# Attention before a routed MoE: factors and gates taken from PSUM tile by tile, tail maxima from transposes, heads of a pair in turn, and a planner that knows a shared port

## The chip, the cores and the metric

One core of a Trainium2 chip runs the whole program in one launch. The metric is the device time in microseconds (us) of that core, as the median of the runs. Five engines work side by side and meet at semaphores: PE (TensorE, matmuls and transposes), DVE (VectorE), ACT (ScalarE), POOL (GpSimd) and SP (SyncE, which here only issues DMAs, one after the other). PE and the transposes write PSUM; the other data lies in SBUF.

## The reference, cut to what matters

```
q, k, v: (8, 8, 576, 64)                 # batch, head, position, width
q_s = softmax(q, axis=-1)                # exp(q - max) / sum over the width
k_s = softmax(k, axis=2)                 # exp(k - max) / sum over the positions
kv  = einsum('bhsd,bhse->bhde', k_s, v)
x   = einsum('bhsd,bhde->bhse', q_s, kv) # then reshaped to 4608 tokens x 512
logits = x @ w_gate                      # 8 experts; every token goes to one, 576 per expert, best logits first
out = relu(x[mask] @ w1[e]) @ w2[e]      # per expert
h = out @ w_in; g = h * tanh(softplus(h)); result = g @ w_out
```

## The kernel before, in words

The program has three stages, each with an order of its own that a planner, `Sched`, writes out before anything runs. Every piece of work is an `op` with an engine, a cost in us, the keys it reads and writes, the buffers it takes (`new`) and a priority. `run` simulates the engines: it takes again and again the op that can start first (the priority settles ties), and emits it. So each engine's queue is in the planned order, and on the chip each engine works strictly down its queue. SP's DMA issues are planned in the same way, as engine "DMA".

Stage one is `attention`, with routing for the first expert at its end. Stage two runs the eight experts, stage three the last two matrices. The change is in `Sched`, in `attention`, in one flag of `route` and in three costs of `load_x`.

`attention` goes over the 8 batches b. Of the 576 positions of a head, 512 lie as 128 partitions x 4 rows r; the last 64 (the tail) of two batches share one tile. For each batch:

- `k_side`: `mx1` (L238, DVE) takes the maximum over the four rows of k, in two halves of 4 heads. `mx2` (L243, DVE) joins the tail's values, SBUF with SBUF, on 64 partitions. `tr` (PE) transposes, `red` (L253, DVE) reduces to the maximum over the partitions, `bc` (PE) spreads it, `cp` (ACT) copies it to SBUF. `sub` and `subh` (L269, L274, POOL) subtract it from k and `ex`, `exh` (ACT) take exp in place.
- `kv_side`: `mm` multiplies k with v for each head h, main part (L322) and tail (L315). Even heads write PSUM partitions 0 to 63, odd heads 64 to 127. The main loop does all four rows of one head, then those of the next. `norm` (L329 to L335, DVE) divides by the sums, `tr` (L341), `cp` and `gate` (L350) multiply by the gate's weights, so that KV has 128 columns of values, 16 of gates and 2 that give q's sums.
- `q_side`: `mx` (L374, DVE), `sub` (L380, POOL) and `ex` (ACT) for q. Then 36 tiles of 128 tokens, 4 a batch and one more for each pair of tails: `tr` (L394, PE), `cp` (L403, ACT) to `xs`, `mm` (L410, L413, PE) into the PSUM tile `xp`, of which there are two. `take` (L420, ACT) copies the 18 columns of gates and sums to SBUF and `copy` (L441, ACT) the 128 x 4 values to `xs`. When all four tiles of a group are there, `logits` makes the factor R (L426 add, L427 reciprocal), multiplies the gates by it (L429) and sums them into L (L433), all on DVE. `scaled` (L437) multiplies `xs` by R in place, the 18 odd tiles on DVE and the 18 even ones on POOL; `store` (L446, L450) sends two tiles at a time to DRAM (`xd`).

The PSUM tag "mT" has two buffers for everything but the q tiles and xp. k has 3 buffers, q three half-batch ones. All loads and stores are issued by SP in planned order, so a store that waits for its tiles holds the loads behind it.

The routing of the first expert (`route`, `round`) takes L in three pieces (tiles 0 to 17, 18 to 29, 30 to 35; `sel_first`, L625 on, `digits`, `cmp` L833), then six rounds of counting between DVE and PE. POOL then issues the indirect loads of the first expert's weights (L901) and the gathers of its tokens from `xd` (`load_x`, L929), which PE transposes.

Of the kernel before, what the change touches and what calls it, by code (L numbers as in the profile page):

```python
# [40 lines left out]
class Sched:  # L41
# [8 lines left out]
    def op(self, eng, cost, fn, r=(), w=(), prio=0, new=(), lat=None, slack=0.0):  # L50
# [21 lines left out]
        self.ops.append((eng, cost, fn, deps, prio, [k for _, k in new], lat, slack))  # L72
        return i
# [6 lines left out]
    def run(self, free=()):  # L80
# [17 lines left out]
        def start(i, t):  # L98
            s = max(t, free.get(self.ops[i][0], 0.0))
            for k in self.ops[i][5]:  # L100
                a = avail[self.kind[k]]
                if not a:
                    return None
                s = max(s, min(a))
            return s

        while ready:
# [4 lines left out]
            if self.keep and self.ops[i][4] >= self.urgent and self.ops[i][0] in ("DVE", "ACT"):  # L112

                end = key[i][0] + self.keep * self.ops[i][1]
                soon = [key[j] for j in key if self.ops[j][0] == self.ops[i][0] and self.ops[j][4] < self.urgent
                        and key[j][0] < end]
                if soon:
                    i = min(soon)[2]
            s = key[i][0]
            eng, cost, fn, deps, prio, new, lat, _ = self.ops[i]  # L120
# [6 lines left out]
            free[eng] = e  # L127
            done = e + (lat if lat is not None else 2.53 if eng == "DMA" else self.lat)
# [13 lines left out]
def attention(tc, nc, cst, q, k, v, w_gate, xs, L, R, xd, route):  # L142
# [12 lines left out]
            "qT": 2, "xp": 2, "km": 1, "dg": 2, "ms": 3, "gs": 3}  # L155
    sc = Sched(SLOT, 0.298)
# [21 lines left out]
    def load_k(b):  # L178
# [10 lines left out]
        for hh in range(2):  # L189
            sc.op("DMA", 1.5, lambda hh=hh: part(hh), w=[("k", b, hh)] + ([("kk", b)] if hh == 0 else []),  # L190
                  new=[("k", ("kk", b))] if hh == 0 else [], prio=0)
# [3 lines left out]
    def load_v(b):  # L195
# [13 lines left out]
        for hh in range(2):  # L209
            sc.op("DMA", 1.9, lambda hh=hh: part(hh), w=[("v", b, hh)] + ([("vv", b)] if hh == 0 else []),  # L210
                  new=[("v", ("vv", b))] if hh == 0 else [], prio=0)
# [3 lines left out]
    def load_q(b):  # L215
# [10 lines left out]
        for hh in range(2):  # L226
            sc.op("DMA", 1.5, lambda hh=hh: part(hh), w=[("q", b, hh)], new=[("q", ("q", b, hh))], prio=0)
# [4 lines left out]
    def k_side(b):  # L232
# [54 lines left out]
        for hh in range(2):  # L287
            sc.op(DVE, 1.25, lambda hh=hh: mx1(hh), r=[("k", b, hh), kk], w=[km], new=[("km", km)] if hh == 0 else [], prio=p)
        sc.op(DVE, 0.72, mx2, r=[kh, km], w=[km, khx], prio=p)
        sc.op(PE, 0.45, tr, r=[km], w=[mT], new=[("mT", mT)], prio=p)  # L290
        sc.op(DVE, 0.72, red, r=[mT], w=[dg], new=[("dg", dg)], prio=p)
        sc.op(PE, 0.45, bc, r=[dg], w=[mb], new=[("mT", mb)], prio=p)
        sc.op(ACT, 0.62, cp, r=[mb], w=[ms], new=[("ms", ms)], prio=p)
        for hh in range(2):
            sc.op(POOL, 2.45, lambda hh=hh: sub(hh), r=[ms, kk, ("k", b, hh)], w=[("k", b, hh)], prio=p)
            sc.op(ACT, 1.08, lambda hh=hh: ex(hh), r=[kk], w=[("k", b, hh)], prio=p)
        sc.op(POOL, 1.45, subh, r=[ms, kh, khx], w=[khx], prio=p)
# [3 lines left out]
    def kv_side(b):  # L301
# [5 lines left out]
        def mm(h0, h1, tail):  # L307
# [3 lines left out]
            for h in range(h0, h1):  # L311
                a, i = h % 2, h // 2
                c = slice(a * 64, a * 64 + 64)
                if tail:
                    nc.tensor.matmul(pt[c, i, 1:66], T["kh", b // 2][o:o + 64, h, :],  # L315
                                     T["vh", b // 2][o:o + 64, h, :], start=False, stop=(h >= 6),
                                     skip_group_check=True)
                    continue

                for r in range(4):  # L320
                    at = (0, 65, 129, 194)[r]
                    nc.tensor.matmul(pt[c, i, r % 2:r % 2 + 65], T["k", b, h // HH][:, h % HH, r, :],  # L322
                                     T["v", b, h // HH][:, h % HH, at:at + 65],
                                     start=(h == a and r == 0), stop=False, skip_group_check=True)
# [42 lines left out]
    def q_side(b):  # L367
# [47 lines left out]


        def take(r, r0, n):
            if r == r0:
                T["gs", b, r0] = wk.tile([128, 4, 4, KVW - 128], F32, name="gs", bufs=3)
            nc.scalar.activation(T["gs", b, r0][:, r - r0], T["xp", b, r][:, :, 128:KVW], AF.Copy)  # L420

        def logits(r0, n):
            g = T["gs", b, r0][:, 0:n]
            j = j_of(r0)
            rs = R[:, j:j + n]
            nc.vector.tensor_scalar(rs, g[:, :, :, 16:18], EPS, None, op0=OP.add)  # L426
            nc.vector.reciprocal(rs, rs)  # L427
            G = wk.tile([128, 4, 8, E], F32, name="G")
            nc.vector.tensor_tensor(G[:, 0:n].rearrange("p r (i a) e -> p (r i) a e", i=4),  # L429
                                    g[:, :, :, 0:16].rearrange("p r i (a e) -> p (r i) a e", a=2),  # L430
                                    rs.rearrange("p r i a -> p (r i) a")[:, :, :, None].to_broadcast([128, 4 * n, 2, E]),
                                    op=OP.mult)
            nc.vector.tensor_reduce(L[:, j:j + n, :], G[:, 0:n].rearrange("p r x e -> p r e x"), axis=AX, op=OP.add)  # L433

        def scaled(eng, r):
            x = part(r).rearrange("p i (a d) -> p (i a) d", a=2)
            eng.tensor_tensor(x, x, R[:, j_of(r)].rearrange("p i a -> p (i a)")[:, :, None].to_broadcast([128, 8, D]),  # L437
                              op=OP.mult)

        def copy(r):  # L440
            nc.scalar.activation(part(r), T["xp", b, r][:, :, 0:128], AF.Copy)  # L441

# [9 lines left out]
        for u in range(2 + b % 2):  # L452
# [3 lines left out]
            sc.op(POOL, 0.4 + 0.8 * n, lambda u=u: sub(u), r=[m], w=[qk], prio=p)  # L456
            sc.op(ACT, 0.2 + 0.45 * n, lambda u=u: ex(u), r=[qk], w=[qe], new=[("qe", qe)], prio=p)
        groups = [(0, 4)] if b < 7 else [(0, 2), (2, 2)]
        for r0, n in groups + [(4, 1)] * (b % 2):
            gs, L_ = ("gs", b, r0), [("L", j_of(r0) + i) for i in range(n)]  # L460
            for r in range(r0, r0 + n):
# [6 lines left out]
                sc.op(ACT, 0.26, lambda r=r, r0=r0, n=n: take(r, r0, n), r=[xp], w=[gs], new=[("gs", gs)] if r == r0 else [],  # L468
                      prio=p + 3.11)
                sc.op(ACT, 0.62, lambda r=r: copy(r), r=[xp], w=[x], prio=p + 3.74)  # L470
            sc.op(DVE, 0.6 + 0.2 * n, lambda r0=r0, n=n: logits(r0, n), r=[gs], w=[("R", b, r0)] + L_, prio=p + 3.11)
            for r in range(r0, r0 + n):
                x = ("x", b, r)
                if j_of(r) % 2:
                    sc.op(DVE, 0.75, lambda r=r: scaled(nc.vector, r), r=[("R", b, r0)], w=[x], prio=1000)
                else:
                    sc.op(POOL, 1.1, lambda r=r: scaled(nc.gpsimd, r), r=[("R", b, r0)], w=[x], prio=1000)
            for s0 in range(r0, r0 + n, 2):
                m = min(2, n)
                sc.op("DMA", 0.7 * m, lambda s0=s0: store(s0), r=[("x", b, r) for r in range(s0, s0 + m)], prio=3000)  # L480
# [104 lines left out]
class Moe:  # L585
# [17 lines left out]
    def route(self, ph, bank):  # L603
# [7 lines left out]
        def dve(cost, fn, r=(), w=(), early=False, slack=0.0):  # L611
            sc.op("DVE", cost, fn, r=[(x, ph) if isinstance(x, str) else x for x in r],
                  w=[(x, ph) if isinstance(x, str) else x for x in w], prio=0 if early else p, slack=slack)
# [309 lines left out]
    def load_x(self, ph, xd):  # L923
# [28 lines left out]
        for t in range(5):  # L952
            n = 128 if t < 4 else 64
            xg, tp, xt = ("xg", ph, t), ("tp", ph, t), ("xt", ph, t)
            sc.op("POOL", 1.1, lambda t=t, n=n: gather(t, n), r=[("ix", ph), "xd"], w=[xg], new=[("xg", xg)],
                  prio=p, lat=5.0 if ph else 2.5, slack=0.0 if ph else LISTS)
            sc.op("PE", 0.45, lambda t=t, n=n: tr(t, n), r=[xg], w=[tp], new=[("tp", tp)] if ph or t == 4 else [], prio=p)
# [672 lines left out]
```

## Time and profile before

| what | us |
|---|---|
| three runs | 1448.83, 1460.53, 1455.08; median 1455.08 |
| the profiled execution | 1457.38 |
| its span, first to last instruction | 1455.6 |

Busy shares over the span: PE 93%, DVE 74%, ACT 55%, POOL 19%. The profile's page cuts the span in 40 slices of some 36 us; the attention is the first four and a half. The windows view gives the same busy times for chosen stretches, the groups view sums instructions of a line, the timeline lists instructions in order with the idle time before each and what ended it. A row of the groups reads: line, engine, operation, output and inputs, count | busy us, mean ns | idle before.

### The profile page before, as it was taken

The page shows a single profiled execution, that of the slowest core. Times are in us where ns is not written, and L with a number is a line of the kernel's source. Part 1 is how long each engine was busy: PE and PEld are TensorE (multiplying, and loading weights), DVE is VectorE, ACT ScalarE, POOL GpSimd, SP SyncE. Part 2 cuts the span into 40 slices and gives each one's busy share as a digit, 9 for nine tenths or more (in the row PEclk, how much of TensorE's full clock was granted, in tenths as well). Part 3 has the DMA queues.
Part 4 walks back from the last instruction along what each step waited for, and adds up shares of the span by engine and source line. Part 5 has one row for each costly group of instructions (what it writes and reads, how often), then busy time and mean ns, then how long its engine had stood idle before and what let it go on. Part 6 is the DMA issues. An engine that isn't in the chain of part 4 may idle for free.

```text
span 1455.6 us, 26681 instructions
## 1 busy us (share of the span) xinstructions
PE 1350.2 (93%) x10240; PEld 1249.3 (86%) x10240; DVE 1073.7 (74%) x2144; ACT 798.8 (55%) x1558; POOL 273.0 (19%) x305
## 2 busy tenths in 40 slices
PE   4779469799999998999899999999999999999997
PEld 3668469699899997999799899998989999999896
DVE  8888876688688776763878677777768677786764
ACT  3458332343444435542766666666667666666663
POOL 8567241232232132100001000010101001010101
PEclk9899779899999998999999999999999999999999
DMA  9985442464565649767876566675657656665650
GB/s 274 226 232 175 166 149 90 129 187 147 159 225 163 201 151 301 251 211 266 301 275 207 170 222 190 201 239 168 208 177 250 200 164 215 196 226 175 192 178 29
DMA packets 161919, 286.98 MB, mean 197 GB/s; under 512 B 25600, under 2 KB 101376, under 8 KB 161792
## 3 DMA queue, kind: packets, MB, share of 16 engines
q1 hardware_dynamic: 137680, 222.35, 49.4%
q0 software_dynamic: 15040, 52.44, 10.9%
q10 hardware_dynamic: 9072, 10.49, 2.1%
q8 instruction: 81, 1.33, 0.4%
q14 instruction: 46, 0.38, 0.1%
HBM read 235.95 MB, written 49.28 MB: 196 GB/s over the span
## 4 chain that ended last, share of the span: by engine, by line
PE 44%; issue 39%; DVE 7%; DMA 4%; POOL 3%; ACT 2%; SPq 1%; another core or an unknown queue 0%; ACTq 0%; POOLq 0%; DVEq 0%
PE hp L971 13%; PE yp L990 13%; PE yp L1456 5%; PE hp L1330 5%; POOL out_dram L1468 2%; PE rt L845 2%; PE xp L410 1%; DMA wst<-in_moe_w_dram,wi 1%; PE kvp L322 1%; PE tp L940 1%; DVE km L238 1%; DMA wdi<-unit 1%; DVE G L429 1%; DMA yst<-yd 1%; PE qT L394 1%
## 5 line engine op out<-in xcount | busy, mean ns | idle before, releaser
L1456 PE MATMUL yp<-unit,g 128*128 128x512 f32 x1728 | 431.3, 392 | 0.1
L1456 PEld LDWEIGHTS yp<-unit,g 128*128 128x128 f32 x1728 | 309.9, 188 | 56.4 <-DVE g L1368 1.0
L1330 PEld LDWEIGHTS hp<-yTa,unit 128*128 128x128 f32 x2256 | 288.3, 188 | 18.6 <-DVE hp L1419 2.9
L1330 PE MATMUL hp<-yTa,unit 128*128 128x256 f32 x2256 | 294.1, 279 | 4.1 <-DVE hp L1419 2.7
L971 PE MATMUL hp<-xT,unit 128*128 128x288 f32 x1536 | 281.3, 303 | 7.8 <-DVE hh L982 7.6
L990 PE MATMUL yp<-hh,unit 128*128 128x288 f32 x1500 | 264.3, 297 | 0.5 <-issue 0.4
L971 PEld LDWEIGHTS hp<-xT,unit 128*128 128x128 f32 x1536 | 228.7, 191 | 9.4 <-DVE hh L982 8.2
L990 PEld LDWEIGHTS yp<-hh,unit 128*128 128x128 f32 x1500 | 220.8, 189 | 1.3 <-issue 0.9
L1468 POOL DMA_INDIRECT out_dram<-os,gix x36 | 39.5, 1098 | 786.8 <-ACT os L1464 453.7
L978 ACT ACTIVATE hh<-hp 128x288 fp32r<-128x288 f32 x125 | 51.1, 409 | 211.0 <-PE hp L971 179.3
L1338 ACT ACTIVATE u<-hp 128x512 f32<-128x512 f32 x144 | 85.9, 597 | 117.0 <-PE hp L1330 111.3
L1355 DVE SCALAR_TENSOR_TENSOR u<-w,r 128x512 f32<-128x512 f32 x144 | 98.8, 687 | 45.4 <-ACT r L1352 44.8
L1365 ACT ACTIVATE g<-w 128x512 fp32r<-128x512 f32 x144 | 90.3, 628 | 75.0 <-DVE w L1361 73.1
L901 POOL DMA_INDIRECT wst<-in_moe_w_dram,wi x64 | 67.7, 1058 | 277.8 <-DVE unit L888 76.3
L882 ACT ACTIVATE unit<-wst 128x512 fp32r<-128x512 f32 x128 | 77.7, 646 | 54.4 <-DMA wst<-in_moe_w_dram,wi 48.3
L982 DVE SCALAR_TENSOR_TENSOR hh<-hp,hh 128x288 fp32r<-128x288 f32 x125 | 56.7, 455 | 64.2 <-ACT hh L978 60.9
L1368 DVE TENSOR_TENSOR g<-w,g 128x512 fp32r<-128x512 f32 x144 | 98.8, 686 | 5.6 <-ACT g L1365 3.5
L1361 DVE SCALAR_TENSOR_TENSOR w<-r,hp 128x512 f32<-128x512 f32 x144 | 98.3, 684 | 5.5
L1330 PEld LDWEIGHTS hp<-yTb,unit 128*128 128x128 f32 x768 | 99.1, 191 | 3.6
L1330 PE MATMUL hp<-yTb,unit 128*128 128x256 f32 x768 | 102.1, 282 | 0.0
L1358 DVE SCALAR_TENSOR_TENSOR r<-u,r 128x512 f32<-128x512 f32 x144 | 98.8, 687 | 1.9
L1341 DVE TENSOR_SCALAR u<-u 128x512 f32<-128x512 f32 x144 | 61.2, 427 | 50.9 <-ACT u L1338 50.1
(203 smaller groups left out, 1767.9 us busy)
## 6 DMA issues: line engine op xcount, KB each, us to landing
unit<-wdi SPq DMA_DIRECT2D x216, 512.0 KB
unit<-wdi SPq DMA_DIRECT2D x72, 256.0 KB
wdi<-unit SPq DMA_DIRECT2D x56, 256.0 KB
yd<-ys ACTq DMA_DIRECT2D x15, 576.0 KB
k<-in_k_dram SPq DMA_DIRECT2D x16, 512.0 KB
q<-in_q_dram SPq DMA_DIRECT2D x16, 512.0 KB
v<-in_v_dram SPq DMA_DIRECT2D x32, 256.0 KB
xd<-xs SPq DMA_DIRECT2D x16, 512.0 KB
```

What stands on the lines that cost most here:

```text
L882: nc.scalar.activation(f, v, AF.Copy)
L971: MM(t, u[:, a, 128 * (f % 4):128 * (f % 4) + 128], x[:, b, k, HALF * hf:HALF * hf + HALF], start=(k == 0 and n == 0), stop=(k == 3 and n ...
L990: MM(T["yp", ph, hf][d], u[:, a, 128 * d:128 * d + 128], t[:, b], start=(f == 0 and n == 0), stop=(f == 7 and n == 2))
L1330: MM(dst, u[:, h, a, kk], y[:, b, kk], start=first, stop=False, skip_group_check=True)
L1338: nc.scalar.activation(t, T[zp], AF.Exp)
L1355: V.scalar_tensor_tensor(T[u], T[w], 1.0, T[rk], op0=OP.add, op1=OP.mult)
L1358: V.scalar_tensor_tensor(T[rk], T[u], 2.0, T[rk], op0=OP.subtract, op1=OP.mult)
L1361: V.scalar_tensor_tensor(T[w], T[rk], 0.5, T[zp], op0=OP.add, op1=OP.mult)
L1365: nc.scalar.activation(t[:, 0], T[w], AF.Copy)
L1368: V.tensor_tensor(T[g][:, 1], T[w], T[g][:, 0].bitcast(F32), op=OP.subtract)
L1456: MM(T["op", c, t], g[:, a, 128 * t:128 * t + 128], u[:, b], start=(i == 0 and n == 0), stop=(i == 15 and n == 2))
L1468: at = nc.gpsimd.indirect_dma_start(out=out, out_offset=bass.IndirectOffsetOnAxis(ap=gix[:, 4 * c + t:4 * c + t + 1], axis=0), in_=T["os", ...
```

## The change

Seven edits:

1. `take` moves from ACT to DVE and does a tile at a time, straight from PSUM: factor (add, reciprocal) and gates times factor, into a tile `G`. `logits` is only the sum.
2. The tiles whose number is a multiple of 4 (9 of 36) are also scaled by `take`, PSUM to `xs`, with no ACT copy. The other 27 are copied by ACT and scaled on POOL, none on DVE.
3. `mx2` is gone. Once per pair of batches PE transposes the tail tile (`trh`, buffer of tag "mT") and DVE reduces it (`redh`); `red` gets a second, small reduction over the two maxima.
4. `mm` of k and v takes the two heads of a pair in turn, row by row.
5. Stores of `xd` wait for the last batch's loads to have been issued and landed.
6. In `Sched`, ops marked `port` (POOL's subtractions and scalings, DVE's early routing) exclude each other in the plan, DVE and ACT ops may wait for a much more urgent one, and costs are corrected (`mx1` 1.25 to 1.95, loads 1.5 to 1.75, `mm` 2.0 to 1.1).
7. The last batch's tiles form groups (0, 1) and (2, 3, 4), the latter with priority -950; in `load_x` the first expert's gathers and transposes have other planned costs.

```diff
@@ Sched.run
+            if self.ops[i][8]:
+                s = max(s, free.get("port", 0.0))
...
-            if self.keep and self.ops[i][4] >= self.urgent and self.ops[i][0] in ("DVE", "ACT"):
+            limit = self.ops[i][4] - 500 if self.urgent is None else self.urgent
+            if self.keep and self.ops[i][4] >= limit and self.ops[i][0] in ("DVE", "ACT"):
...
+            if port:
+                free["port"] = e
@@ attention
-    sc = Sched(SLOT, 0.298)
+    sc = Sched(SLOT, 0.298, 1.0, None)
@@ k_side
-        def mx2():
-            m, o = T["km", b], (b % 2) * 64
-            nc.vector.tensor_tensor(m[o:o + 64], m[o:o + 64], T["kh", b // 2][o:o + 64], op=OP.max)
+        def trh():
+            t = T["hT", b // 2] = ps.tile([128, 4, 128], F32, name="hT", tag="mT", bufs=2)
+            m = T["kh", b // 2]
+            for i in range(4):
+                nc.tensor.transpose(t[:, i, :], m[:, 2 * i:2 * i + 2, :].rearrange("p a d -> p (a d)"), ident)
+        def redh():
+            t = T["m2", b // 2] = wk.tile([128, 4, 2, 2], F32, name="m2")
+            nc.vector.tensor_reduce(t[:, :, :, 1], T["hT", b // 2].rearrange("p i (o t) -> p i o t", o=2), axis=AX, op=OP.max)
...
-            nc.vector.tensor_reduce(t, T["mT", b], axis=AX, op=OP.max)
+            m = T["m2", b // 2][:, :, b % 2]
+            nc.vector.tensor_reduce(m[:, :, 0], T["mT", b], axis=AX, op=OP.max)
+            nc.vector.tensor_reduce(t, m, axis=AX, op=OP.max)
@@ kv_side
-            for h in range(h0, h1):
-                a, i = h % 2, h // 2
...
-                for r in range(4):
+            for i in range(h0 // 2, h1 // 2):
+                for r in (range(4, 5) if tail else range(4)):
+                    for a in range(2):
+                        h, c = 2 * i + a, slice(a * 64, a * 64 + 64)
@@ q_side
+        def early(r):
+            return j_of(r) % 4 != 0
-        def take(r, r0, n):
-            nc.scalar.activation(T["gs", b, r0][:, r - r0], T["xp", b, r][:, :, 128:KVW], AF.Copy)
+        def take(r, r0):
+            xp, rs = T["xp", b, r], R[:, j_of(r)]
...
+            V.tensor_scalar(rs, xp[:, :, 144:146], EPS, None, op0=OP.add)
+            V.reciprocal(rs, rs)
+            for o, at, n in ([] if early(r) else [(part(r), 0, D)]) + [(T["G", b, r0][:, r - r0], 128, E)]:
+                V.tensor_tensor(o if n == E else o.rearrange("p i (a d) -> p i a d", a=2),
+                                xp[:, :, at:at + 2 * n].rearrange("p i (a d) -> p i a d", a=2),
+                                rs[:, :, :, None].to_broadcast([128, 4, 2, n]), op=OP.mult)
...
-                if j_of(r) % 2:
-                    sc.op(DVE, 0.75, lambda r=r: scaled(nc.vector, r), r=[("R", b, r0)], w=[x], prio=1000)
+                if early(r):
+                    sc.op(ACT, 0.62, lambda r=r: copy(r), r=[xp], w=[x], prio=p + 3.74)
+                    sc.op(DVE, 0.55, lambda r=r, r0=r0: take(r, r0), r=[xp, G][:1 + (r > r0)], w=w, new=new, prio=first)
+                    sc.op(POOL, 1.1, lambda r=r: scaled(r), r=[rk], w=[x], prio=1000, port=True)
                 else:
-                    sc.op(POOL, 1.1, lambda r=r: scaled(nc.gpsimd, r), r=[("R", b, r0)], w=[x], prio=1000)
+                    sc.op(DVE, 1.25, lambda r=r, r0=r0: take(r, r0), r=[xp, G][:1 + (r > r0)], w=w + [x], new=new, prio=first)
...
-                sc.op("DMA", 0.7 * m, lambda s0=s0: store(s0), r=[("x", b, r) for r in range(s0, s0 + m)], prio=3000)
+                sc.op("DMA", 0.7 * m, lambda s0=s0: store(s0), r=[("x", b, r) for r in range(s0, s0 + m)]
+                      + [("in", B - 1, x, hh) for x in "kqv" for hh in range(2)], prio=3000)
```

## Rows read from the trace of the kernel before

**Rows 1.** Windows: us, busy (x) of PE, PEld, DVE, ACT, POOL; PEclk, DMA, GB/s.
```profile
6.00:70.00 64.00, 40.21 (x400) 35.61 (x400) 53.48 (x56) 26.87 (x46) 46.98 (x37) 0.87 1.15 267
6.00:163.50 157.50, 116.69 (x1279) 105.28 (x1279) 136.05 (x185) 91.36 (x176) 107.87 (x75) 0.92 0.85 223
163.50:204.50 41.00, 14.86 (x184) 12.19 (x185) 30.56 (x95) 8.64 (x16) 11.28 (x12) 0.56 0.50 164
204.50:1455.00 1250.50, 1218.61 (x8784) 1131.79 (x8780) 903.09 (x1835) 697.57 (x1366) 149.17 (x180) 0.99 0.61 195
```

**Rows 2.** Groups by line, DVE, from 6 to 163.5 us.
```profile
L238 DVE TENSOR_REDUCE km<-k 128x256 f32<-128x1024 f32 x16 | 30.7, 1942 | 4.9 <-DMA k<-in_k_dram 4.8
L429 DVE TENSOR_TENSOR G<-gs,R 128x256 f32<-128x256 f32 (+2 forms) x13 | 20.8, 1600 | 0.4
...
L437 DVE TENSOR_TENSOR xs<-xs,R 128x512 f32<-128x512 f32 x15 | 15.1, 1027 | 0.0
L243 DVE TENSOR_TENSOR km<-km,kh 64x512 f32<-64x512 f32 x8 | 9.1, 1132 | 0.2
L335 DVE TENSOR_TENSOR KV<-kvp,ks 64x256 f32<-64x256 f32 x16 | 6.8, 423 | 0.5
...
L426 DVE TENSOR_SCALAR R<-gs 128x32 f32<-128x32 f32 (+2 forms) x13 | 6.2, 476 | 2.7 <-ACT gs L420 2.7
L253 DVE TENSOR_REDUCE mx<-mT 128x4 f32<-128x512 f32 x8 | 5.5, 692 | 5.3 <-PE mT L249 4.9
L427 DVE RECIPROCAL R<-R 128x32 f32<-128x32 f32 (+2 forms) x13 | 3.8, 291 | 0.4
...
L329 DVE TENSOR_SCALAR ks<-kvp 128x8 f32<-128x8 f32 x8 | 1.3, 163 | 2.1 <-PE kvp L315 2.0
```

**Rows 3.** Timeline of DVE: start, us, engine, line, operation; stalled and free instances.
```profile
51.45 7.44 DVE L429 TENSOR_TENSOR G<-gs,R 128x256 f32<-128x256 f32 x1
...
80.95 5.69 DVE L429 TENSOR_TENSOR G<-gs,R 128x256 f32<-128x256 f32 x1
...
131.05 0.20 DVE L427 RECIPROCAL R<-R 128x8 f32<-128x8 f32 x1
131.29 0.23 DVE L429 TENSOR_TENSOR G<-gs,R 128x64 f32<-128x64 f32 x1
...
148.81 0.43 DVE L429 TENSOR_TENSOR G<-gs,R 128x256 f32<-128x256 f32 x1
```

**Rows 4.** Timeline of POOL, beside the second of those stalls.
```profile
81.69 4.67 POOL L269 TENSOR_TENSOR k<-k,ms 128x1024 f32<-128x1024 f32 x2
```

**Rows 5.** Timeline of PE: the two long gaps, and a main and a tail product.
```profile
65.26 1.09 PE L341 MATMUL kT<-ident,KV 128*128 128x128 f32 x4 [9.20 <-DVE KV L335]
...
97.23 1.09 PE L341 MATMUL kT<-ident,KV 128*128 128x128 f32 x4 [7.08 <-DVE KV L335]
...
114.65 1.55 PE L322 MATMUL kvp<-v,k 128*64 128x65 f32 x32
...
116.72 0.68 PE L315 MATMUL kvp<-vh,kh 64*64 64x65 f32 x16
```

**Rows 6.** SP's queue: its waits (total us, times, longest), and the last load issued.
```profile
SPq L219 <- ACT qe L387: 32.1, 10, 10.1
SPq L446 <- DVE xs L437: 19.7, 7, 5.7
...
135.51 0.38 SPq L219 DMA_DIRECT2D q<-in_q_dram  x1
```

**Rows 7.** Timeline of DVE where the last piece of routing begins.
```profile
163.34 0.68 DVE L437 TENSOR_TENSOR xs<-xs,R 128x512 f32<-128x512 f32 x1
...
167.14 0.35 DVE L833 TENSOR_TENSOR cm<-x,tab 128x384 bf16<-128x384 bf16 x1
```

**Rows 8.** Group by line, POOL, from 6 to 163.5 us.
```profile
L437 POOL TENSOR_TENSOR xs<-xs,R 128x512 f32<-128x512 f32 x18 | 20.4, 1150 | 10.7 <-DVE R L427 4.1 <-PE qT L394 3.4 <-ACT xs L403 2.1
```

**Rows 9.** Timeline of POOL: its first issue after the attention.
```profile
185.18 1.17 POOL L901 DMA_INDIRECT wst<-in_moe_w_dram,wi  x1 [22.58 <-DVE rk L706]
```

More of the change, by code (lines that the diff above doesn't have):

```diff
@@ L48, in __init__, with op @@
         self.touch, self.kind = {}, {}
-    def op(self, eng, cost, fn, r=(), w=(), prio=0, new=(), lat=None, slack=0.0):
+    def op(self, eng, cost, fn, r=(), w=(), prio=0, new=(), lat=None, slack=0.0, port=False):
         i = len(self.ops)
@@ L71, in op @@
         deps.discard(i)
-        self.ops.append((eng, cost, fn, deps, prio, [k for _, k in new], lat, slack))
+        self.ops.append((eng, cost, fn, deps, prio, [k for _, k in new], lat, slack, port))
         return i
@@ L119, in run @@
             s = key[i][0]
-            eng, cost, fn, deps, prio, new, lat, _ = self.ops[i]
+            eng, cost, fn, deps, prio, new, lat, _, port = self.ops[i]
             del ready[i]
@@ L189, in load_k @@
         for hh in range(2):
-            sc.op("DMA", 1.5, lambda hh=hh: part(hh), w=[("k", b, hh)] + ([("kk", b)] if hh == 0 else []),
+            sc.op("DMA", 1.75, lambda hh=hh: part(hh), w=[("in", b, "k", hh), ("k", b, hh)] + ([("kk", b)] if hh == 0 else []),
                   new=[("k", ("kk", b))] if hh == 0 else [], prio=0)
@@ L209, in load_v @@
         for hh in range(2):
-            sc.op("DMA", 1.9, lambda hh=hh: part(hh), w=[("v", b, hh)] + ([("vv", b)] if hh == 0 else []),
+            sc.op("DMA", 1.9, lambda hh=hh: part(hh), w=[("in", b, "v", hh), ("v", b, hh)] + ([("vv", b)] if hh == 0 else []),
                   new=[("v", ("vv", b))] if hh == 0 else [], prio=0)
@@ L226, in load_q @@
         for hh in range(2):
-            sc.op("DMA", 1.5, lambda hh=hh: part(hh), w=[("q", b, hh)], new=[("q", ("q", b, hh))], prio=0)
+            sc.op("DMA", 1.75, lambda hh=hh: part(hh), w=[("in", b, "q", hh), ("q", b, hh)], new=[("q", ("q", b, hh))], prio=0)
         if b % 2 == 1:
@@ L435, in scaled @@
[L435 to L438, printed above, removed]
+                T["G", b, r0] = wk.tile([128, 4, 4, 2, E], F32, name="G", bufs=3)
+            V = nc.vector
+            V.tensor_scalar(rs, xp[:, :, 144:146], EPS, None, op0=OP.add)
[4 more added lines that the diff above has]
+                                rs[:, :, :, None].to_broadcast([128, 4, 2, n]), op=OP.mult)
@@ L440, in copy, with scaled @@
+        def logits(r0, n):
+            nc.vector.tensor_reduce(L[:, j_of(r0):j_of(r0) + n, :],
+                                    T["G", b, r0][:, 0:n].rearrange("p r i a e -> p r e (i a)"), axis=AX, op=OP.add)
         def copy(r):
             nc.scalar.activation(part(r), T["xp", b, r][:, :, 0:128], AF.Copy)
+        def scaled(r):
+            x = part(r).rearrange("p i (a d) -> p (i a) d", a=2)
+            nc.gpsimd.tensor_tensor(x, x, R[:, j_of(r)].rearrange("p i a -> p (i a)")[:, :, None].to_broadcast([128, 8, D]),
+                                    op=OP.mult)
@@ L455, in q_side @@
             sc.op(DVE, 0.16 + 0.54 * n, lambda u=u: mx(u), r=[qk], w=[m], prio=p)
-            sc.op(POOL, 0.4 + 0.8 * n, lambda u=u: sub(u), r=[m], w=[qk], prio=p)
+            sc.op(POOL, 0.3 + 0.82 * n, lambda u=u: sub(u), r=[m], w=[qk], prio=p, port=True)
             sc.op(ACT, 0.2 + 0.45 * n, lambda u=u: ex(u), r=[qk], w=[qe], new=[("qe", qe)], prio=p)
-        groups = [(0, 4)] if b < 7 else [(0, 2), (2, 2)]
-        for r0, n in groups + [(4, 1)] * (b % 2):
-            gs, L_ = ("gs", b, r0), [("L", j_of(r0) + i) for i in range(n)]
+        groups = [(0, 4)] + [(4, 1)] * (b % 2) if b < 7 else [(0, 2), (2, 3)]
+        for r0, n in groups:
+            first = -950 if (b, r0) == (7, 2) else p + 3.11
+            L_ = [("L", j_of(r0) + i) for i in range(n)]
             for r in range(r0, r0 + n):
@@ L467, in q_side @@
                       new=[("xp", xp)], prio=p)
[L468 to L473, printed above, removed]
-                if j_of(r) % 2:
-                    sc.op(DVE, 0.75, lambda r=r: scaled(nc.vector, r), r=[("R", b, r0)], w=[x], prio=1000)
-                else:
-                    sc.op(POOL, 1.1, lambda r=r: scaled(nc.gpsimd, r), r=[("R", b, r0)], w=[x], prio=1000)
+                rk, G = ("R", b, r), ("G", b, r0)
+                new, w = [("G", G)] if r == r0 else [], [G, rk] if r == r0 else [("G", b, r0, r), rk]
+                if early(r):
+                    sc.op(ACT, 0.62, lambda r=r: copy(r), r=[xp], w=[x], prio=p + 3.74)
+                    sc.op(DVE, 0.55, lambda r=r, r0=r0: take(r, r0), r=[xp, G][:1 + (r > r0)], w=w, new=new, prio=first)
+                    sc.op(POOL, 1.1, lambda r=r: scaled(r), r=[rk], w=[x], prio=1000, port=True)
+                else:
+                    sc.op(DVE, 1.25, lambda r=r, r0=r0: take(r, r0), r=[xp, G][:1 + (r > r0)], w=w + [x], new=new, prio=first)
+            sc.op(DVE, 0.06 + 0.15 * n, lambda r0=r0, n=n: logits(r0, n), r=[("G", b, r0)] + [("G", b, r0, r) for r in range(r0 + 1, r0 + n)],
+                  w=L_, prio=first)
             for s0 in range(r0, r0 + n, 2):
-                m = min(2, n)
-                sc.op("DMA", 0.7 * m, lambda s0=s0: store(s0), r=[("x", b, r) for r in range(s0, s0 + m)], prio=3000)
+                m = min(2, r0 + n - s0)
+                sc.op("DMA", 0.7 * m, lambda s0=s0: store(s0), r=[("x", b, r) for r in range(s0, s0 + m)]
+                      + [("in", B - 1, x, hh) for x in "kqv" for hh in range(2)], prio=3000)
     def setup():
@@ L612, in dve @@
             sc.op("DVE", cost, fn, r=[(x, ph) if isinstance(x, str) else x for x in r],
-                  w=[(x, ph) if isinstance(x, str) else x for x in w], prio=0 if early else p, slack=slack)
+                  w=[(x, ph) if isinstance(x, str) else x for x in w], prio=0 if early else p, slack=slack, port=early)
         def pe(cost, fn, r=(), w=(), new=()):
```

58 lines of the change are left out of this document (24 added, 34 removed).

## The prediction

> **What bounds the kernel now.** I read the windows first, because the page's shares are a mean over three stages. From 204.5 us to the end PE is busy 1218.6 of 1250.5 us at a granted clock of 0.99 [rows 1]: nothing of the change is in there, so that stretch should move as a block. What can be won lies before it. From 163.5 to 204.5 runs the first routing, a chain between DVE and PE with neither full. From 6 us (the first k has landed) to 163.5 (the last logits are made) DVE is busy 136.1 of 157.5 us, PE 116.7, POOL 107.9, ACT 91.4 [rows 1]. So the attention is DVE's, with 21.4 us of idle time. The loads are close behind: up to 70 us the DMA engines are full, at 267 GB/s [rows 1].
>
> Then the groups of DVE in that stretch [rows 2], against single instances in the timeline [rows 3]. The product of gates and factors, L429, takes 20.8 us in 13 pieces; one of 128x256 took 7.44 us, another 5.69, a free one 0.43. What the long instances share is POOL: the 5.69 one runs from 80.95 to 86.64 and beside it POOL subtracts, without a break, from 81.69 to 86.36 [rows 4]. L335, of like size but with one input in PSUM, averages 0.42 over 16, so none of its instances was held long [rows 2]. A DVE operation with both tensors in SBUF waits for POOL's subtractions; one that reads PSUM does not. L426, L437 and L243 read SBUF alone and have means of 0.48, 1.03 and 1.13 [rows 2].
>
> Next PE's timeline, for what a stall does outside DVE. The two long L429 are followed by PE's longest gaps in the attention, 9.20 and 7.08 us, both ended by KV from L335, which stood in DVE's queue behind the stall [rows 5]. Last SP's queue: it waits 32.1 us for ACT to free q buffers and 19.7 us at stores of x for L437 on DVE, and the last q half is issued only at 135.5 [rows 6].
>
> **The change, part by part.** The sum is made on DVE's time in 6 to 163.5 us.
>
> Removed: L429 20.8, L426 6.2, L427 3.8, L437 15.1 and L243 9.1 us, together 55.0 [rows 2]. The sum into L stays as it is.
>
> Added by `take`, 36 times: an add from PSUM as L329 does it (0.16) [rows 2], a reciprocal of 128x8 (0.20) and a product of 128x64 [rows 3]. The trace has that product only from SBUF, 0.23 free [rows 3]; from PSUM the nearest is L335, four times as long a row on half the partitions, 0.42 [rows 2]. The term therefore lies between 36 x 0.59 = 21.2 and 36 x 0.78 = 28.1. I take 0.26, near the row of the same size: 36 x 0.62 = 22.3.
>
> Added for the 9 tiles scaled from PSUM: a pass over 128x512 of PSUM, L253's 0.69 [rows 2]: 6.2. Added for the tails: four reductions of 128x512 from PSUM, 4 x 0.69, and eight tiny ones at 0.16 (L329's, the smallest) [rows 2]: 4.1.
>
> Net on DVE: 55.0 - 22.3 - 6.2 - 4.1 = 22.4 us less. All that is added reads PSUM or is too short to meet POOL often, so I count no stalls in it. Bounds: with the dear product 16.6; above, one cannot tell how much of DVE's 21.4 us of idle goes too. It waits for transposes and late loads, and these wait for DVE. With half of it gone the gain is 33.
>
> Moved to PE: four transposes per pair, four times. One such set takes at most 1.09 us here (those right after a gap) [rows 5], so up to 4.4 us. Against it stands the order of heads. A main half is 32 instructions in 1.55 us, 48 ns each; the tail, which already takes the columns 0 to 63 and 64 to 127 in turn, 16 in 0.68, 43 ns each [rows 5]. In turn the half would cost 32 x 43 = 1.36, 0.19 less, 3 us in 16 halves; nothing is the other end. PE has 41 us of slack in the stretch [rows 1], so I cost PE's part at zero. The cover is DVE's load; were it gone, it would be 4.4 against 3.
>
> ACT loses 36 small copies and 9 large ones and is no bound. The stores behind all loads free SP from its 19.7 us at L446 [rows 6]; q loads then start earlier. I count 1 us, for DVE's idle time at late q only; the bounds are 0 and the half of the idle above. The stores themselves come late, in one run, but the first gather stands behind POOL's weight loads, which begin more than 20 us after the last logits [rows 9]. What they queue behind on SP is loads alone.
>
> After the last logits, three L437 stand between the routing's steps from 163.34 to 167.14 [rows 7]. They go: 3 x 0.60 (start to start) = 1.8.
>
> The planner's edits make no instruction cheaper. `mx1` was booked at 1.25 and takes 1.94 [rows 2], so the planned order was early by 0.7 us sixteen times over; a truer order serves the idle term, which I leave at nothing beyond that 1 us. The three costs in `load_x` move the order of the experts' stage: between -3 and +3, taken as 0, since PE is full there.
>
> Sum: 22.4 + 1.8 + 1.0 = 25.2 us. From the profiled 1457.4 that gives 1432.2; the median of the runs is 2.3 below the profiled execution, so 1430.
>
> **The rivals.**
>
> *POOL becomes the bound.* Nine more tiles of 1.15 us [rows 8] make 10.4 us. POOL's weight loads and gathers stand behind the scalings in its queue, and what it has not scaled by then it does beside the routing, whose SBUF operations wait for it as L429 did. For it: if POOL's 49.6 us of idle (157.5 - 107.9) stay, it ends at 163.5 + 10.4 = 173.9, while its first weight load, now at 185.2 [rows 9], is wanted at 160: 14 us late, 1444. Against it: most of that idle is spent waiting for DVE. The Trainium skill speaks against this edit: "GPSIMD Engine Reference", "Key points", has DVE about twice as fast on elementwise work, and says that the engines share SBUF interfaces, with contention for DVE instructions with two SBUF inputs. On the second the stalled L429 agrees; on the first the free L437 of 0.68 stands against POOL's 1.15 [rows 7, 8], 1.7 times.
>
> *The loads hold the end.* The last q half is issued at 135.5 because q buffers come free late [rows 6]. If that chain is not DVE's but its own, only the 28 us behind it shrink, by DVE's share 22.4 / 136: 4.6 + 1.8 = 6.4, 1449. Against it: ACT frees q after POOL's subtraction, which waits for DVE's maximum.
>
> *More than forecast.* DVE's idle time halves with the stalls: 33 + 1.8, 1420.
>
> *Slower: xp waits for DVE.* ACT emptied the gates from the two PSUM tiles; now DVE must, standing in a queue with the 1.94 us maxima [rows 2], and PE, in order, holds k's products behind the xp that finds no tile. If each of 36 tiles waits half a maximum, 0.97, that is 35 us on PE against 25 won: 10 slower, 1465. It decides from 0.7 us a tile. Against it: the plan places the takes with that wait in view, and DVE has less to do than before.
>
> *The turns of heads bring nothing.* The half stays at 1.55: no change in the sum, as PE has slack.
>
> **How the numbers follow.** A run can be told from no change here from about 1% (14.5 us). Forecast 0.62, own range 1420 to 1440; POOL 0.15 (half of it over the 1% line); loads 0.10 (over 6 us won, partly over 14.5); more than forecast 0.08; slower 0.05. Faster by over 1%: 0.60 + 0.07 + 0.06 + 0.08 = 0.81; slower 0.04; the rest, 0.15, within 1%. The range reaches from some 8 us below the 1420 case to just past POOL's: 1412 to 1446. It leaves out most of the loads case and the slower one.
>
> **What would show it.** Right: no DVE product over 1 us beside POOL but in the early routing; PE without gaps of 7 or 9 us; `take` at some 0.6 us a tile; the last logits near 139 us; the last q issued well before 135; the stretch from the first expert's products to the end still about 1250 us. Wrong: POOL still scaling when the routing's rounds begin, or its first weight load waiting for POOL itself; PE idle before L410 until DVE's take; or an experts' stage whose length has changed by over 5 us, since I count that as fixed.

## The result and the profile after

The changed kernel takes 1435.39 us (median of 6, 1432.10 to 1436.88) against 1454.76 for the kernel before (6 runs, the three of the table before and the profiled one among them): a ratio of 0.986, interval 0.9834 to 0.9885. The same kernel run again later gave 0.9863 (0.9835 to 0.9890). Forecast were 1430, in 1412 to 1446. The profiled execution is 1433.58 us, 23.8 under the profiled one of before; the sum had said 25.2.

The windows of the changed kernel, cut at the same events as [rows 1]: first k landed, last logits made, start of the experts' main stretch.

```profile
6.00:70.00 64.00, 48.24 (x557) 42.87 (x558) 49.13 (x78) 37.49 (x57) 52.05 (x41) 0.95 1.08 273
6.00:138.10 132.10, 109.54 (x1289) 98.67 (x1289) 106.70 (x236) 82.61 (x131) 111.02 (x82) 0.97 1.03 274
138.10:181.40 43.30, 15.06 (x190) 12.15 (x191) 32.76 (x104) 7.75 (x15) 11.56 (x13) 0.57 0.40 131
181.40:1431.50 1250.10, 1220.02 (x8779) 1133.36 (x8777) 902.57 (x1833) 699.12 (x1368) 149.82 (x180) 0.99 0.62 195
```

The attention went from 157.5 to 132.1 us, 25.4 less; the stretch behind it from 41.0 to 43.3; the rest stayed. DVE's busy time fell from 136.1 to 106.7 and its idle time rose, from 21.4 to 25.4. POOL, with 111 of 132 us, is now the busiest of the four.

DVE's groups in that window answer to [rows 2]:

```profile
L244 DVE TENSOR_REDUCE km<-k 128x256 f32<-128x1024 f32 x16 | 31.3, 1967 | 0.6 <-DMA k<-in_k_dram 0.3
...
L447 DVE TENSOR_TENSOR G<-xp,R 128x64 f32<-128x64 f32 x36 | 8.0, 221 | 0.9
L445 DVE RECIPROCAL R<-R 128x8 f32<-128x8 f32 x36 | 7.3, 203 | 1.2
L354 DVE TENSOR_TENSOR KV<-kvp,ks 64x256 f32<-64x256 f32 x16 | 6.8, 422 | 0.4
L447 DVE TENSOR_TENSOR xs<-xp,R 128x512 f32<-128x512 f32 x9 | 6.2, 691 | 0.5
...
L444 DVE TENSOR_SCALAR R<-xp 128x8 f32<-128x8 f32 x36 | 5.9, 163 | 9.6 <-PE xp L429 6.3 <-ACT xs L456 2.0 <-PE xp L432 1.3
...
L256 DVE TENSOR_REDUCE m<-hT 128x8 f32<-128x512 f32 x4 | 2.8, 692 | 2.5 <-PE hT L252 2.4
...
L268 DVE TENSOR_REDUCE mx<-m 128x4 f32<-128x8 f32 x8 | 1.3, 160 | 0.3
```

The three steps of a take sum to 0.59 us a tile, and no mean hides a stall: 36 products from PSUM at 0.22, where the group products of before took 20.8 us in 13 pieces.

PE's timeline, beside [rows 5]:

```profile
32.95 1.09 PE L252 MATMUL hT<-ident,kh 128*128 128x128 f32 x4 [3.83 <-DMA kh<-in_k_dram]
...
71.91 0.66 PE L360 MATMUL kT<-ident,KV 128*128 128x128 f32 x4 [0.34 <-DVE KV L354]
...
79.17 1.15 PE L341 MATMUL kvp<-v,k 128*64 128x65 f32 x32
...
97.88 0.63 PE L360 MATMUL kT<-ident,KV 128*128 128x128 f32 x4 [1.06 <-DVE KV L354]
```

The gaps of 9.20 and 7.08 us before `kT` are gone (the longest two now: 1.06 and 1.02). A new wait is there: the tails' transposes stand in PE's queue until their load lands. SP's queue, beside [rows 6]:

```profile
104.05 0.64 SPq L225 DMA_DIRECT2D q<-in_q_dram  x1
104.74 4.54 SPq L466 DMA_DIRECT2D xd<-xs  x4
```

The last q half is issued 31 us earlier. The stores start right behind it, before its data is used (DVE still waits for it up to 110.87): that stores wait for the last loads to have landed holds in the plan only. Where the attention hands over to the routing, on DVE, beside [rows 7]:

```profile
137.59 0.49 DVE L452 TENSOR_REDUCE L<-G 128x24 f32<-128x192 f32 x1
138.12 0.20 DVE L648 TENSOR_REDUCE v<-L 128x6 f32<-128x48 f32 x1
138.36 1.09 DVE L652 TENSOR_TENSOR t<-L,v 128x48 bf16<-128x48 f32 x1
...
141.41 0.24 DVE L648 TENSOR_REDUCE v<-L 128x12 f32<-128x96 f32 x1
...
143.84 0.56 DVE L856 TENSOR_TENSOR cm<-x,tab 128x768 bf16<-128x768 bf16 x1
```

The scalings between the routing's steps are gone. But the second piece (12 tiles) runs after the third (6 tiles); before, it lay ahead of the last logits. Its 3 us, 141.4 to 144.4, are most of why the stretch behind the attention grew. The rest is L652, which stands beside POOL's last scaling and takes 1.09 us, 0.9 more than the same step of the kernel before; less the 1.8 of the scalings that makes 2.1 of the 2.3. That step before the change:

```profile
164.17 0.21 DVE L629 TENSOR_TENSOR t<-L,v 128x48 bf16<-128x48 f32 x1
```

POOL, beside [rows 9]:

```profile
138.35 1.04 POOL L460 TENSOR_TENSOR xs<-xs,R 128x512 f32<-128x512 f32 x1 [0.70 <-ACT xs L456]
162.05 1.17 POOL L924 DMA_INDIRECT wst<-in_moe_w_dram,wi  x1 [22.66 <-DVE rk L729]
```

Its last scaling ends 1.3 us after the last logits; the weight loads wait for the routing, not for POOL.

### The profile page after: what moved, and what is told of

Its sections match the earlier page's. It is cut to its first block, busy times and chain, and to the rows that moved or that the text cites. A ratio compares the mean times of both kernels' runs of the same rounds, so it can differ in the third digit from the quotient of the medians.

```text
span 1431.8 us, 26732 instructions
## 1 busy us (share of the span) xinstructions
PE 1344.6 (94%) x10256; PEld 1244.2 (87%) x10256; DVE 1046.1 (73%) x2207; ACT 790.8 (55%) x1513; POOL 277.1 (19%) x314
## 4 chain that ended last, share of the span: by engine, by line
PE 55%; issue 30%; DMA 5%; DVE 5%; POOL 2%; ACT 2%; SPq 1%; ACTq 0%; POOLq 0%; DVEq 0%
PE hp L994 13%; PE yp L1013 12%; PE yp L1479 12%; PE hp L1353 11%; PE rt L868 2%; DMA kh<-in_k_dram 2%; POOL out_dram L1491 2%; DMA wst<-in_moe_w_dram,wi 2%; PE tp L963 1%; PE xp L429 1%; DMA xg<-xd,ix 1%; DVE km L244 1%; DMA v<-in_v_dram 1%; DMA q<-in_q_dram 0%; DVE cm L856 0%
## 5 line engine op out<-in xcount | busy, mean ns | idle before, releaser
L994 PE MATMUL hp<-xT,unit 128*128 128x288 f32 x1536 | 284.7, 303 | 4.2 <-DVE hh L1005 3.5
L1001 ACT ACTIVATE hh<-hp 128x288 fp32r<-128x288 f32 x125 | 51.3, 411 | 199.3 <-PE hp L994 183.3
```

What stands on the lines that cost most here:

```text
L994: MM(t, u[:, a, 128 * (f % 4):128 * (f % 4) + 128], x[:, b, k, HALF * hf:HALF * hf + HALF], start=(k == 0 and n == 0), stop=(k == 3 and n ...
```

## The experiments

All start from the changed kernel. Times of single stages are from one profile each. Three profiles with one and the same order of instructions, the changed kernel, its control and u_stores (see there), put the last logits at 138.1, 137.3 and 140.9 and the first expert product at 176.8, 176.5 and 179.8, so differences under some 4 us show nothing. x_psum, x_sbuf, u_plan and u_stores ran on one chip, the other experiments on a second one; the kernel before took 1461.98 us on the first and 1455.15 or 1452.87 on the second, so the ratios are the fairer measure.

| kernel | last logits, us | first expert product, us | ratio to before |
|---|---|---|---|
| before | 163.4 | 199.9 | 1 |
| changed | 138.1 | 176.8 | 0.986 (0.9834 to 0.9885) |
| u_take | 163.2 | 199.3 | 0.9984 (0.9963 to 1.0004) |
| u_take_port | 143.3 | 190.0 | 0.9939 (0.9920 to 0.9957) |
| u_tail | 139.5 | 177.3 | 0.9862 (0.9844 to 0.9881) |
| u_heads | 138.4 | 177.6 | 0.9866 (0.9849 to 0.9884) |
| x_psum | 138.9 | 178.0 | one run |
| x_sbuf | 156.5 | 195.5 | one run |
| u_plan | 143.7 | 178.8 | 0.9889 (0.9853 to 0.9924) |
| u_stores | 140.9 | 179.8 | 0.9867 (0.9840 to 0.9894) |
| v_less | 138.5 | 177.7 | one run |
| f_cut | 140.1 | 176.3 | 0.9879 (0.9854 to 0.9905) |
| f_cut3 | 142.7 | 178.9 | 0.9885 (0.9853 to 0.9916) |
| again (control) | 137.3 | 176.5 | 0.9863 (0.9835 to 0.9890) |

**u_take: factors and gates by group from SBUF again.**

```diff
-            V.tensor_scalar(rs, xp[:, :, 144:146], EPS, None, op0=OP.add)
+            nc.scalar.activation(T["gs", b, r0][:, r - r0], T["xp", b, r][:, :, 128:KVW], AF.Copy)
...
+                if j_of(r) % 2:
+                    sc.op(DVE, 0.75, lambda r=r: scaled(nc.vector, r), r=[("R", b, r0)], w=[x], prio=1000)
```

> The changed kernel with one part undone: gates and sums are copied to SBUF by ACT again, factors and gates are made for a whole group from SBUF, and 18 tiles are scaled on DVE in SBUF; the rest of the change stays, the planner's too, but it is not told that these DVE operations need the port. Theory (stalls of DVE operations with both tensors in SBUF beside POOL's subtractions): the group products of 128x256 take several us again where POOL works, DVE's busy time from 6 us to the last logits is 20 us or more above the changed kernel's 106.7, and the last logits come 12 to 25 us later than 138.1. Rival (the planner's order brought the gain, and the memory of the operands matters little): the products stay under 1 us and the last logits come within 5 us of 138.

Undoing this part (edits 1 and 2 together; no run separates them) undoes the whole gain: last logits at 163.2. The window up to there, with DVE busy 130.4 us against 106.7, and groups of DVE in it:

```profile
6.00:163.20 157.20, 121.67 (x1295) 110.92 (x1295) 130.37 (x180) 92.12 (x176) 107.62 (x74) 0.88 0.84 221
```

```profile
L244 DVE TENSOR_REDUCE km<-k 128x256 f32<-128x1024 f32 x16 | 31.0, 1956 | 1.8 <-DMA k<-in_k_dram 1.6
L455 DVE TENSOR_TENSOR xs<-xs,R 128x512 f32<-128x512 f32 x14 | 21.1, 1547 | 0.0
...
L444 DVE TENSOR_SCALAR R<-gs 128x32 f32<-128x32 f32 (+3 forms) x12 | 9.2, 766 | 7.4 <-ACT gs L438 7.3
L447 DVE TENSOR_TENSOR G<-gs,R 128x256 f32<-128x256 f32 (+3 forms) x12 | 7.7, 642 | 0.4
```

In one detail the expectation failed: the group products are not the long ones now (mean 0.64). The order differs, and the stalls fell on the scalings, 1.55 us a piece, and on the additions. Which SBUF product or addition meets POOL depends on the order; not every SBUF operation is held: the maxima of L244 take 1.96 us here as in the other kernels. The last q half leaves 17 us later than in the changed kernel:

```profile
121.50 0.37 SPq L225 DMA_DIRECT2D q<-in_q_dram  x1
```

**u_take_port: the same, with the planner told.**

```diff
-    sc.op(DVE, 0.6 + 0.2 * n, lambda r0=r0, n=n: logits(r0, n), r=[gs], w=[("R", b, r0)] + L_, prio=first)
+    sc.op(DVE, 0.6 + 0.2 * n, lambda r0=r0, n=n: logits(r0, n), r=[gs], w=[("R", b, r0)] + L_, prio=first, port=True)
```

(and the same on DVE's scalings.)

> As the kernel before it in this list, but the planner is told that the group products and the scalings on DVE exclude POOL's work. Theory (the stall itself costs, and PSUM is the way round it): told or not, DVE and POOL still need each other's time, so what DVE does not stall it waits in the plan: last logits 8 to 25 us after 138.1. Rival (knowing the port is enough): last logits within 5 us of 138.1 with the old products.

Each view has half. The last logits come 5.2 us late only, so a plan that keeps the two engines apart recovers 20 of 25 us, and making factors for a whole group, which this kernel shares with u_take, costs at most those 5.2 at the last logits. But what it kept apart it put off: twelve scalings ran on DVE between 150.9 and 171.9, during the routing, and the stores behind them. SP's queue:

```profile
157.62 14.89 SPq L464 DMA_DIRECT2D xd<-xs  x8
172.61 2.70 SPq L468 DMA_DIRECT2D xd<-xs  x2
```

and POOL's first gather of `xd`, which needs them all (the wait named is another DMA of that queue; the stores are what it reads):

```profile
180.97 0.95 POOL L950 DMA_INDIRECT xg<-xd,ix  x1 [11.45 <-DMA w<-in_moe_w_in_dram]
```

In the changed kernel that gather comes at 167.9. So of the 19.9 us that the plan won over u_take at the last logits, 9.3 are left at the first expert product (190.0 against 199.3).

**x_psum and x_sbuf: one product more in each take, equal but for the memory of one operand.**

```diff
+            V.tensor_tensor(wk.tile([128, 4, 2, E], F32, name="twice", bufs=1), xp[:, :, 128:144].rearrange("p i (a d) -> p i a d", a=2),
+                            rs[:, :, :, None].to_broadcast([128, 4, 2, E]), op=OP.mult)
```

In x_sbuf `wgbd`, of the same shape in SBUF, stands for `xp[:, :, 128:144]`.

> The changed kernel, same plan, with one more product in every take: the same 128x64 product of xp (PSUM) and factors, written a second time to a scratch tile that nobody reads. Both theories: 36 more of about 0.22 us, 8 us more of DVE busy time, last logits 0 to 5 us after 138.1. It is the control of the next kernel.

> The same with the scratch product's first operand in SBUF (the gate weights, the same shape), so that only the memory of one operand differs from the kernel before. Theory (a DVE operation with both tensors in SBUF waits for POOL's subtractions and scalings, and POOL is busy 111 of 132 us): the scratch products have a mean of 0.7 us or more where POOL works, DVE's busy time grows by over 20 us, and the last logits come 8 to 30 us after 138.1. Rival (the stalls came from something else, such as the broadcast factor): 0.22 us as in the control, and the same end.

The group of the added product in x_psum:

```profile
L450 DVE TENSOR_TENSOR twice<-xp,R 128x64 f32<-128x64 f32 x36 | 7.7, 213 | 0.0
```

and in x_sbuf:

```profile
L450 DVE TENSOR_TENSOR twice<-wgbd,R 128x64 f32<-128x64 f32 x36 | 28.5, 793 | 0.0
```

Same plan, same size, same count: 0.21 against 0.79 us. Single instances take 0.211 to 0.218 us in x_psum and 0.212 to 2.477 in x_sbuf. The end moves by 0.8 us in the one and by 18.4 in the other. The windows of both up to their last logits, x_psum first:

```profile
6.00:138.90 132.90, 109.33 (x1289) 98.21 (x1289) 110.53 (x272) 82.68 (x131) 111.02 (x82) 0.97 1.04 272
```

```profile
6.00:156.50 150.50, 119.26 (x1289) 107.24 (x1289) 131.08 (x273) 83.45 (x131) 111.20 (x82) 0.90 0.92 241
```

DVE's busy time grew by 24.4 us in x_sbuf, as expected, but by 3.8 in x_psum and not by 8: in the trace the added products partly overlap the instructions beside them. The pair shows the mechanism by itself: the product whose tensors both lie in SBUF waits for POOL, the one with an operand in PSUM does not.

**u_tail: the tails' maxima on DVE from SBUF again.**

```diff
+            nc.vector.tensor_tensor(m[o:o + 64], m[o:o + 64], T["kh", b // 2][o:o + 64], op=OP.max)
...
-            sc.op(PE, 0.45, trh, r=[kh], w=[hT, ("khx", b), ("khx", b + 1)], new=[("mT", hT)], prio=p)
```

> The changed kernel with the tails' maxima joined on DVE from SBUF again (eight of 64x512), no transposes of the tails. Theory by DVE's sum: 9.1 us removed and 4.1 added, so 5 us more busy time on DVE and last logits 2 to 6 us later. Rival (loads and PE set the end by now, DVE has slack): within 1.5 us of 138.1.

The window of u_tail up to the changed kernel's last logits:

```profile
6.00:138.10 132.10, 111.37 (x1264) 98.09 (x1264) 116.01 (x233) 81.72 (x130) 113.02 (x81) 0.96 1.03 273
```

DVE works 9.3 us more, where 5 were expected: the joined maxima cost 9.8 instead of 9.1, 1.9 are steps of the routing's second piece that now run ahead of the last logits, and the rest, on balance, is longer steps of the early routing. The end comes 1.4 us later and the first product 0.5: the rival. This part of the change is not worth anything that can be measured; PE no longer waits for the tails' loads in exchange.

**u_heads: one head after the other.**

```diff
-                for r in (range(4, 5) if tail else range(4)):
-                    for a in range(2):
+                for r, a in [(4, a) for a in range(2)] if tail else [(r, a) for a in range(2) for r in range(4)]:
```

> The changed kernel, same plan, but the products of k and v do all rows of one head before the next head. Theory of the prediction (PE has slack): each half goes from 1.08 back to 1.48 us, 6.4 us of PE in all, and the last logits move by under 1.5 us. Rival (PE, busy 109.5 of 132 us, now lies on the path): last logits 3 to 7 us later.

PE's timeline in u_heads, a main half:

```profile
74.74 1.55 PE L341 MATMUL kvp<-v,k 128*64 128x65 f32 x32
```

Heads in turn make the half 1.15 instead of 1.55 us. In u_heads PE's busy time in the window is 113.6 against 109.5, and the end moves by 0.3 us: nothing.

**u_plan: the planner without the port and without the wait for urgent operations.**

```diff
-    sc = Sched(SLOT, 0.298, 1.0, None)
+    sc = Sched(SLOT, 0.298)
...
-            if port:
-                free["port"] = e
```

> The changed kernel with the planner's port exclusion and its waiting for urgent operations taken out, costs and work as changed. Theory (what the chip executes counts; the takes read PSUM, so hardly anything on DVE meets POOL): last logits within 4 us of 138.1, the early routing's operations a little longer. Rival (the planner's knowledge carries the gain): 8 to 25 us later.

Between the two: last logits 5.6 us later. But here the routing's second piece comes before them, on DVE:

```profile
134.46 0.24 DVE L644 TENSOR_REDUCE v<-L 128x12 f32<-128x96 f32 x1
...
143.16 0.50 DVE L448 TENSOR_REDUCE L<-G 128x24 f32<-128x192 f32 x1
```

so the first expert product is only 2.0 us behind the changed kernel's, and the ratios' intervals overlap. Beside u_stores, the changed kernel's order on the same chip, the last logits come 2.8 us later and the first product 1.0 earlier: no effect is shown.

**u_stores: stores free to go among the loads.**

```diff
-                sc.op("DMA", 0.7 * m, lambda s0=s0: store(s0), r=[("x", b, r) for r in range(s0, s0 + m)]
-                      + [("in", B - 1, x, hh) for x in "kqv" for hh in range(2)], prio=3000)
+                sc.op("DMA", 0.7 * m, lambda s0=s0: store(s0), r=[("x", b, r) for r in range(s0, s0 + m)], prio=3000)
```

> The changed kernel with stores of xd free to go among the loads as soon as their tiles are ready. The prediction's step (SP frees 19.7 us, of which 1 us counts): last logits 0 to 2 us later. Rival (loads are the bound by now, 274 GB/s over the whole attention, and stores in between delay them): the last q half is issued 8 us or more after 104, and the last logits come 5 to 15 us later.

The last q load, SP's queue in u_stores:

```profile
105.53 0.45 SPq L225 DMA_DIRECT2D q<-in_q_dram  x1
106.03 4.65 SPq L466 DMA_DIRECT2D xd<-xs  x4
```

The first store still goes behind the last q: no store went among the loads. Instruction by instruction, every engine, SP too, has the order of the changed kernel. With the rest of the change in place the plan puts the stores there without being told, so this run decides neither the step nor the rival. It is a repeat of the changed kernel, and its 2.8 us at the last logits are the spread between repeats.

**v_less: fewer loads.** v is loaded for three batches only, its tails for four; later batches use old values, so the result is another.

```diff
-            for i in range(2):
+            for i in range(2 if b < NV else 0):
                 x = src(v, b, hh)
```

> The changed kernel, same plan, but v is loaded for the first three batches only (tails for the first four); the later batches use what lies in the buffers, so 5.8 of the 28.3 MB of input are not moved and the output is another. Theory (after the change the loads set the pace up to the last q, which lands at 110 us, and the end follows 28 us behind it): the last q half is issued 8 to 20 us earlier than 104 and the last logits come 5 to 15 us earlier than 138.1. Rival (DVE's own sum, as in the prediction, or POOL, 111 of 132 us busy, holds the end): last logits within 3 us of 138.1.

My theory fell. Its window and its last q load (SP's queue):

```profile
6.00:138.10 132.10, 110.62 (x1289) 99.73 (x1289) 106.07 (x236) 82.19 (x131) 111.14 (x82) 0.96 0.82 230
```

```profile
104.23 0.37 SPq L225 DMA_DIRECT2D q<-in_q_dram  x1
```

230 GB/s instead of 274, the last q issued when it was before, last logits at 138.5. What grew is SP's wait for ACT to free q buffers, here in v_less and then in the changed kernel (total us, times, longest):

```profile
SPq L225 <- ACT qe L406: 44.2, 9, 9.8
```

```profile
SPq L225 <- ACT qe L406: 14.9, 7, 5.0
```

The bytes of the loads do not hold the end of the changed kernel; the last q waits for its buffer.

**f_cut and f_cut3: two tries at a faster version.**

```diff
-EARLY = (0, 18, 30, NJ)
+EARLY = (0, 18, 26, NJ)
```

f_cut3 has, besides, `return j_of(r) % 3 != 0` in `early`.

> The changed kernel with the routing's second piece cut at tile 26 instead of 30, so that it is ready one batch earlier and can run before the last logits instead of behind them. Theory (2.5 of the 25 us won before the last logits were lost since the second piece stood behind the third): the time from the last logits to the token lists falls from 29.3 to 27.5 us or less, and the first expert product comes 1.5 to 3 us earlier than in the run of the changed kernel beside it. Rival (its operations then delay the takes, or run beside POOL): within 1 us.

> As the kernel before it, with every third tile instead of every fourth scaled by the take from PSUM: 12 on DVE, 24 on POOL. If POOL is what holds the end (111 of 132 us busy): last logits 1 to 3 us earlier. If the loads do: within 1 us, either way; and if DVE does: 1 to 2 us later.

> The changed kernel itself, as a control on the same chip: a ratio to before of 0.984 to 0.988, last logits at 138 within 1 us.

In f_cut the time from the last logits to the token lists is 26.8 us, in the control 29.5: that part is right. But the last logits, on DVE in f_cut, come 2.8 us later than the control's 137.3:

```profile
139.64 0.50 DVE L452 TENSOR_REDUCE L<-G 128x24 f32<-128x192 f32 x1
```

That fits a second piece that costs the same on either side of them, though 2.8 us is no more than the spread of repeats; the first product moves by 0.2 us. f_cut3 takes 3 tiles from POOL, gives them to DVE and ends the attention 5.4 us later than the control: a new order, from which POOL and DVE cannot be told apart. Neither beats the changed kernel.

## Why the prediction held

**The mechanism** was read right from the stalled and free instances of one line [rows 3, 4], and x_psum against x_sbuf shows it. u_take shows that it carries the gain: with that part undone the end of the attention is where it was before. u_take_port adds that what has to be avoided is the stall: a plan that keeps the two engines apart does most of it in the attention, with the operands in SBUF.

**The added terms** were close. Takes 21.2 us (5.9 + 7.3 + 8.0) against 22.3; the nine passes 6.2 against 6.2; the tails 4.1 against 4.1. The product from PSUM costs what the one from SBUF does when free (0.22 and 0.23); the dear bound of 0.42 was too far.

**DVE's sum as the measure** was right in its result and too simple as a reason. DVE's time fell by 29.4 us, not 22.4. Of the 7 more, 4.0 are the routing's second piece, which left the window, and 1.1 are cheaper takes; two stalled steps of the early routing (L629, L645) lost 2.9 and three others gained 1.9. Against that idle time grew by 4 where I had it shrink by 1. The end of the attention moved by 25.4, forecast 23.4 (22.4 + 1.0): that misses of 7 and 5 us nearly cancel is luck. No run shows the 1.0 for the stores. What counts is not DVE's busy time as such: 9.3 us more of it in u_tail and 3.8 in x_psum moved the end by less than repeats differ, 24.4 in x_sbuf by 18.4. That a stall costs more than even work of the same sum, in that everything queued behind it on DVE holds PE, ACT and POOL, is argued: no run adds as much work without stalls.

**The tail** was the step that failed: "They go: 3 x 0.60 (start to start) = 1.8". They went, but the second piece of the routing slid behind the third (3.0 us), and L652 waited 0.9 for POOL's last scaling; the stretch up to the token lists is 29.5 us against 27.3: 2.2 lost instead of 1.8 won. I had not asked what the group of priority -950 passes in DVE's queue.

**Sum.** By the windows -25.4 + 2.3 (41.0 to 43.3) - 0.7 in the rest = -23.8, forecast -25.2. The medians moved less, by 19.4: the profiled run of before was 2.6 above its six-run median, that of after 1.8 below its own. I took 2.3 off for the former; that, with 1.8 and 1.4 for the sum, makes the 5.4 us between 1430 and 1435.4.

**The edits costed at nothing.** PE's part: right in effect, with the size off (a half fell by 0.40, not 0.19). Stores: 1 us said; u_stores has the same order and cannot test it, so this stays open. The planner: put at about nothing, and u_plan shows no effect. But with SBUF operands telling it which DVE operations need the port moves the last logits by 20 us (u_take against u_take_port): in the attention the two parts of the change largely replace each other, at the first expert product u_take_port is still 13.2 behind the changed kernel.

**The rivals.** POOL: did not decide; its scalings end before the rounds begin at 144.4, and first weight loads wait for DVE. In small it came true: the last scaling ran beside the routing and held L652 for 0.9 us. Loads: the chain behind 135.5 was in good part DVE's; with the stalls back (u_take) the last q leaves at 121.5, without them at 104, and with fewer loads (v_less) at 104 too. *Slower: xp waits for DVE*: ACT waits 8.4 us in eight places for a take to finish, PE hardly; no price.

**Open:** what holds the 138 us now. Less of the loads, more of DVE, more of PE moved it by 0.4, 0.8 and 0.3 us, all within the spread of repeats; each of PE, DVE and POOL is busy for 81 to 84% of the stretch. That the planned order passes the work between them so that none is full would fit, but no run relieved two at once, so this is argued, not shown.

## What to carry to other kernels

Look for one operation whose instances differ by a factor of ten, and ask what runs beside the long ones; if it is GpSimd and the tensors are all in SBUF, read one operand from PSUM, where it was anyway, before moving work between engines. Sum the change on the engine that stalls, but test the sum by adding work there: here 3.8 us more on DVE could not be seen at the end, and 24.4 of stalls cost 18.4. After an edit to a planner, compare the order in the trace before reading the time: u_stores had changed nothing. When the last group of a stage gets priority, check what it overtakes and whether that must then run alone.

## What was not expected of the hardware

The Trainium skill's "GPSIMD Engine Reference", "Key points", names contention between GpSimd and DVE instructions with two SBUF inputs; the trace agrees. Here it costs 0.58 us on a product of 0.21 on average (x_sbuf against x_psum), and up to 7 us where POOL's instructions follow each other closely: the product of 7.44 us [rows 3] ran from 51.45 to 58.89, through these on POOL in the kernel before.

```profile
50.96 1.03 POOL L380 TENSOR_TENSOR qh<-qh,qm 128x512 f32<-128x512 f32 x1
51.96 2.03 POOL L437 TENSOR_TENSOR xs<-xs,R 128x512 f32<-128x512 f32 x2
53.96 4.65 POOL L269 TENSOR_TENSOR k<-k,ms 128x1024 f32<-128x1024 f32 x2
```

The last of these five ended at 58.61, 0.28 us before the product.

Products on the two column halves in turn take 1.15 us per 32 instructions against 1.55 one after the other, at a contraction over all 128 rows; I had inferred 1.36 from the tail. The Trainium skill's "TensorEngine Tiling (Array Packing)", "Theoretical Speedup", has up to 2 times where a dimension is at most 64; the trace has 1.35.
